# A Fourier mixing layer and a leaky-ReLU feed-forward: the down projection by 20 products per 2x4x3 block

## The chip, the cores and the metric

The kernel runs on one core of a Trainium2 chip, in one launch. The metric is device time in microseconds; the kernel before takes 1897.99 us (median of 3 runs, 1897.3 to 1898.26). Below, PE is TensorE (matrix products), DVE VectorE, ACT ScalarE, POOL GpSimd, and SP the engine whose queue issues most transfers.

## The reference

```python
def _attn_ref(x):                      # x: (8, 3008, 256) float32
    X = np.fft.fft(x, axis=1)
    X = np.fft.fft(X, axis=2)
    return X.real.astype(np.float32)

def _moe_ref(x, w_in, w_out):          # x: (24064, 256), w_in: (256, 2048), w_out: (2048, 256)
    h = x @ w_in
    g = np.maximum(0.01 * h, h)
    return (g @ w_out).astype(np.float32)
```

The result of the first, reshaped to (24064, 256), is the input of the second.

## The kernel before

**Mixing.** The real part of a two-dimensional Fourier transform has symmetries, so for each batch b only a quarter of the frequencies is made by matrix products. `fold_x` adds and subtracts mirrored rows and columns of x on DVE, `fold_rows` splits rows once more (with turns by `angle` on ACT and DVE), `even_rows` and `odd_rows` multiply by cosine and sine tables on PE, and `butterfly` puts the parts together on DVE. The result of a unit (batch b, parity c) are two tiles `mix0` and `mix1`, the cosine and the sine part, of 752 or 753 frequencies each (`UW`). The Fourier transform along the features is folded into w_in once, which gives `wf` (`fold_w_in`), with the weights of one frequency apart in `wn`; that frequency is spread over all partitions in `nb` (`spread`).

**Up.** A unit is cut into 3 blocks of 250 or 251 columns, 48 blocks in all. A step (j, f) takes block j and two of the 16 feature blocks of 128 (f and 8 + f). `raised` (line 820) does 4 matmuls, into PSUM tiles `cos_ps` and `sin_ps`. `activate` adds wn x nb to the cosine part (line 829), then makes cosine + sine and cosine - sine (lines 833 and 834), which belong to two mirrored output columns, all on DVE, and applies the leaky ReLU on ACT (line 835). So a block of 251 columns gives 502 output columns.

**Down.** The first two blocks (`plain = 2`) are multiplied by w_out in the plain way (`down_plain`, line 873), while the weights are still being converted from float64. From the third on, a step is a 2x2x2 block product by 7 products in place of 8: `combine_w_out` makes 4 sums of weights once, the four GpSimd instructions of lines 842 to 845 make 4 sums of the hidden values per step, and `down` does 7 matmuls (line 893) that accumulate over the 8 steps of the block into 7 halves of PSUM banks. At the end of the block, ACT copies one and DVE puts out four results by 7 additions (line 917), and two transfers store them.

**Order.** In the start, up to step 15, the order of all engines is written out by hand (`manual_schedule`). From step 23 on only DVE's is, and for the other engines program order, with a lag of 3 steps between up and down, sets the priorities. `fold_x`, `fold_rows`, `dft` and `spread` for the next unit are hung onto steps by the tables `folds`, `row_folds` and `transforms`.

PSUM has 8 banks: 4 turn round as `up` (also used by the transforms), 4 as `sum`.

Of the kernel before, what the change touches and what calls it, by code (L numbers as in the profile page):

```python
# [16 lines left out]
P = 128  # L67
# [3 lines left out]
NT = 8  # L71
# [24 lines left out]
SLOPE = 0.01  # L96
# [148 lines left out]
def chunks():  # L245


    out, at = [], 0
    for b in range(B):
        for c in PARITIES:  # L250
            for j in range(0, UW[c], CW):
                n = min(CW, UW[c] - j)
                out.append((b, c, j, n, at))
                at += 2 * n
    return out, at


def columns():

    at = np.zeros(B * S, np.int64)  # L260
    for b, c, j, n, first in chunks()[0]:
        col = j + np.arange(n)
        half, k = col >= KW[c], k_order(c)
        k = np.concatenate([k, k[k != Q]])[col]
        plus, minus = np.where(half, H + k, k), np.where(half, H - k, (S - k) % S)
        at[b * S + minus] = first + n + np.arange(n)
        at[b * S + plus] = first + np.arange(n)
    return at
# [3 lines left out]
def tile_fnet_leaky_relu(  # L272
# [16 lines left out]
    PS = bass.MemoryType.PSUM  # L289
    const = ctx.enter_context(tc.tile_pool(name="const", bufs=1))  # L290
    xp = ctx.enter_context(tc.tile_pool(name="xp", bufs=1))
    work = ctx.enter_context(tc.tile_pool(name="work", bufs=1))
    dram = ctx.enter_context(tc.tile_pool(name="dram", bufs=1, space=bass.MemoryType.DRAM))
    ps = ctx.enter_context(tc.tile_pool(name="ps", bufs=1, space=PS))

    def up_ps(name="up_ps"):
        return ps.tile([P, 512], F32, tag="up", bufs=4, name=name)

    def dft_ps():
        return up_ps("dft_ps")  # L300

    def x_tile():
        return xp.tile([LOADED, 2, 2, NT, D], F32, tag="x", bufs=1, name="xt")

    def sum_ps():
        return ps.tile([P, 512], F32, tag="sum", bufs=4, name="sum_ps")

    def load_x(b):
        t = x_tile()
        for h in range(2):  # L310
            for odd in range(2):
                load_rows(t, b, h, odd)
        return t

    def load_rows(t, b, h, odd):
        nc.sync.dma_start(t[:, h, :, odd * NI[0] : NI[0] + odd * NI[1]], x[b, h, odd])
# [4 lines left out]

    zs = {}
# [22 lines left out]
    def fold_x(b, at):  # L345

        t, rows = xs[b], slice(0, NT)
        h, i = divmod(at, 2)
        if h < 2 and i == 0:
            add_mirrors(t, h, rows)  # L350
        elif h < 2:
            for part in range(2):
                fold_columns(t, h, part, rows)
        else:
            fold_halves(t, i, 3 - h, rows)
        if at == 7:
            zs[b] = xs.pop(b)

    def turn(x, y, a, part, tmp, to, v):
# [3 lines left out]
        nc.scalar.activation(tmp[0], y, ACT.Copy, scale=sin)  # L363
        nc.scalar.activation(tmp[1], y, ACT.Copy, scale=cos)
        if v is nc.vector:
            v.scalar_tensor_tensor(to[0], in0=x, scalar=cos, in1=tmp[0], op0=ALU.mult, op1=op[part])
            v.scalar_tensor_tensor(to[1], in0=x, scalar=sin, in1=tmp[1], op0=ALU.mult, op1=op[1 - part])
            return
        nc.scalar.activation(to[0], x, ACT.Copy, scale=cos)
        nc.scalar.activation(to[1], x, ACT.Copy, scale=sin)  # L370
# [3 lines left out]
    class Rows:  # L374
# [3 lines left out]
        def __init__(self, src, scratch, part, c):  # L378
            self.src, self.scratch, self.part, self.c = src[0:ROWS], scratch, part, c

        def z(self, i, n=None):

            block = 16 // len(self.scratch)
# [3 lines left out]
        def fold_even(self, v=nc.vector):  # L387
            x, y, z = self.src[:, 2], self.src[:, 3], self.z
            if self.c == 1:
                turn(x, y, 0, self.part, (z(0), z(1)), (z(6), z(7)), v)  # L390
# [6 lines left out]
        def fold_odd(self, v=nc.vector):  # L397
            x, y, z = self.src[:, 4:6], self.src[:, 6:8], self.z
            if self.c == 1:
                for i in range(2):  # L400
                    turn(x[:, i], y[:, i], 1 + i, self.part, (z(2 + 2 * i), z(3 + 2 * i)), (z(8 + 2 * i), z(9 + 2 * i)), v)
# [3 lines left out]
            else:  # L405
# [5 lines left out]
                turn(z(b), z(b + 1), 0, self.part, (z(8), z(9)), (z(10), z(11)), v)  # L411
                self.odd = z(7 - self.part), z(6 + self.part), z(10), z(11)

    def rows_of_x(b, part, c):

        t = zs[b]
        src = t[:, (c + part) % 2, 0, :, part * P : (part + 1) * P]
        return Rows(src, [t[:, part, 1].rearrange("p c (i d) -> p (c i) d", i=2)], part, c)

    class Direct:  # L420
# [14 lines left out]
        def odd_rows(self, m, lo=0, hi=KW[1]):  # L435

            po, n = dft_ps() if m == P else sum_ps(), KW[1]
# [26 lines left out]
    rows_of = {}  # L464

    def fold_rows(u, part, odd):
        if not odd:
            rows_of[u, part] = rows_of_x(u[0], part, u[1])
            rows_of[u, part].fold_even()
        else:  # L470
            rows_of[u, part].fold_odd()


    feat_sb = const.tile([P, 2, 2 * P], F32, name="feat_sb")
    wf = const.tile([P, 2, F], F32, name="wf")
    wn = const.tile([P, NF], F32, name="wn")
    wo = const.tile([P, 2, NH, D], F32, name="wo")
    wt = const.tile([P, 4, NH, P], F32, name="wt")
    nyx = const.tile([LOADED, 2, 2, NT, B], F32, name="nyx")
    nyz = const.tile([LOADED, 16, B], F32, name="nyz")  # L480
    nyf = const.tile([LOADED, 2, 2, 2 * FI, B], F32, name="nyf")
# [3 lines left out]
    one = const.tile([1, P], F32, name="one")  # L485
    tabs = {}

    def load_tab(n, c):
        t = const.tile([LOADED, TW[c][n % 2]], F32, name=f"tab_{n}_{c}")
        nc.sync.dma_start(t, seq_tab[n, c, :, 0 : TW[c][n % 2]])  # L490
        tabs[n, c] = t
# [4 lines left out]
    class Weights:  # L496
# [7 lines left out]
        def __init__(self, src, dst):  # L504
            tag = RAW[len(parts)]
            bufs = 1 if tag == "raw" else 2
            words = src.shape[1] * src.shape[2]
            self.raw = work.tile([P, 2 * WN], F32, tag=tag, bufs=bufs, name="raw")[:, 0:words]
            self.dst, self.n = dst, dst.shape[1]
            self.f64 = src.dtype != F32  # L510
            raw = self.raw if not self.f64 else self.raw.bitcast(src.dtype)
            nc.sync.dma_start(raw.rearrange("p (c n) -> p c n", c=src.shape[1]), src)
            parts.append(self)
# [4 lines left out]
        def begin(self):  # L518
# [3 lines left out]
            self.power = work.tile([P, WN], F32, tag="power", bufs=2, name="power")[:, 0 : self.n]  # L522
# [40 lines left out]
    def load_w_in(f0, n, blocks=(0, 1)):  # L563
        words, made = w_in.shape[1] // F, []
        for a in blocks:
            w = work.tile([P, WN], F32, tag="win", bufs=4, name="win")[:, 0:n]
# [4 lines left out]
    def fold_w_in(f0, n, made, tag="up", pieces=1, queue=nc.sync):  # L571


        for w in (1, 0):
            m = n // (1 if w else pieces)
            for at in range(0, n, m):
                pt = ps.tile([P, 512], F32, tag=tag, bufs=4, name="wf_ps")[:, 0:m]
# [12 lines left out]
    def load_w_out(q):  # L590

        src = w_out[q * WB * P : (q + 1) * WB * P, :].rearrange("(c p) d -> p c d", p=P)
        h, f = divmod(q * WB, NH)
        return Weights(src, wo[:, h, f : f + WB, :].rearrange("p c d -> p (c d)"))

    def combine_w_out(f):

        b = [[wo[:, h, f : f + WB, i * P : (i + 1) * P] for i in range(2)] for h in range(2)]
        t = [wt[:, i, f : f + WB, :] for i in range(4)]
        for to, x, y in ((t[0], b[0][1], b[0][0]), (t[1], b[1][1], t[0]), (t[2], b[1][1], b[0][1]), (t[3], b[1][0], t[1])):  # L600
            nc.gpsimd.tensor_tensor(to, x, y, op=ALU.subtract)
# [37 lines left out]
    def butterfly(to, m, part, c, v=nc.vector, direct=False):  # L639
# [4 lines left out]
        def tile_of(tag, w, bufs=1):  # L644
            return work.tile([P, w], F32, tag=tag, bufs=bufs, name=tag)

        if not direct or v is not nc.vector:
            od = tile_of("od", 568)
        if v is nc.vector:
            ab, ev = tile_of("ab", KC), tile_of("ev", KC, 2)  # L650
# [14 lines left out]
        def copied(bank, at, w):  # L665

            a = work.tile([P, 384], F32, tag="e0", bufs=2, name="e0")
            if v is nc.vector:
# [28 lines left out]
        def added(po, lo=0, hi=kw):  # L697
            if c == 0:
                for lo, hi in ((0, 189), (189, kw)):
                    at = lo + (lo > 0)  # L700
                    nc.vector.tensor_tensor(to[0:m, lo:hi], ev[0:m, lo:hi], po[0:m, at : at + hi - lo], op=ALU.add)
                return
            nc.vector.tensor_tensor(to[0:m, lo:hi], ev[0:m, lo:hi], po[0:m, 0 : hi - lo], op=ALU.add)

        def subtracted(po, lo=0, hi=kw):
            if c == 0:

                last = 283
                for lo, hi in ((0, 189), (189, last), (last + 1, kw)):
                    at, first = lo + (lo > 0), kw + lo - (lo > last)  # L710
                    nc.vector.tensor_tensor(to[0:m, first : first + hi - lo], ev[0:m, lo:hi], po[0:m, at : at + hi - lo], op=ALU.subtract)
                return
            nc.vector.tensor_tensor(to[0:m, kw + lo : kw + hi], ev[0:m, lo:hi], po[0:m, 0 : hi - lo], op=ALU.subtract)

        def odd(po):
            if c == 1:
# [4 lines left out]
                v.tensor_tensor(to[0:m, 0:kw], ev[0:m, 0:kw], od[0:m, 0:kw], op=ALU.add)  # L721
                v.tensor_tensor(to[0:m, kw : UW[c]], ev[0:m, 0:kw], od[0:m, 0:kw], op=ALU.subtract)
# [8 lines left out]
            v.tensor_tensor(to[0:m, 0:kw], ev[0:m, 0:kw], od[0:m, 0:kw], op=ALU.add)  # L731

            last = 283
            v.tensor_tensor(to[0:m, kw : kw + last], ev[0:m, 0:last], od[0:m, 0:last], op=ALU.subtract)
            v.tensor_tensor(to[0:m, kw + last : UW[c]], ev[0:m, last + 1 : kw], od[0:m, last + 1 : kw], op=ALU.subtract)
# [3 lines left out]
    def mix(u, blk, direct=False):  # L739

        t = work.tile([P, UW[0]], F32, tag=f"mix{blk}", bufs=2, name=f"mix{blk}")
# [425 lines left out]
```

## Time and profile before

| | |
|---|---|
| median of the runs | 1897.99 us (1897.3 to 1898.26) |
| profiled execution: span | 1895.3 us |
| TensorE busy | 1889.2 us, 100% |
| VectorE busy | 1266.8 us, 67% |
| GpSimd busy | 1055.5 us, 56% |
| ScalarE busy | 501.0 us, 26% |
| TensorE's granted clock | 1.000 of full |
| read from and written to HBM | 52.40 MB and 24.71 MB |

The span runs from the first to the last instruction of one profiled execution. A line of the groups gives source line, engine, operation, output and input tiles, shape and count, then the busy time of the group in us and the mean time of one instruction in ns, then the idle time of the engine ahead of it and what ended it. A line of a timeline begins with start and length in us. Each float32 matmul of this kernel has two records.

### The profile page before, as it was taken

The page shows a single profiled execution, that of the slowest core. Times are in us where ns is not written, and L with a number is a line of the kernel's source. Part 1 is how long each engine was busy: PE and PEld are TensorE (multiplying, and loading weights), DVE is VectorE, ACT ScalarE, POOL GpSimd, SP SyncE. Part 2 cuts the span into 40 slices and gives each one's busy share as a digit, 9 for nine tenths or more (in the row PEclk, how much of TensorE's full clock was granted, in tenths as well). Part 3 has the DMA queues.
Part 4 walks back from the last instruction along what each step waited for, and adds up shares of the span by engine and source line. Part 5 has one row for each costly group of instructions (what it writes and reads, how often), then busy time and mean ns, then how long its engine had stood idle before and what let it go on. Part 6 is the DMA issues. An engine that isn't in the chain of part 4 may idle for free.

```text
span 1895.3 us, 25288 instructions
## 1 busy us (share of the span) xinstructions
PE 1889.2 (100%) x9088; PEld 1682.3 (89%) x9088; DVE 1266.8 (67%) x2543; ACT 501.0 (26%) x674; POOL 1055.5 (56%) x1510
## 2 busy tenths in 40 slices
PE   9999999999999999999999999999999999999999
PEld 7888888988889888898888988889888898888987
DVE  8857765776656776568756687567865677656554
ACT  3522322223222222222222232222322223222222
POOL 0236555565555655556555565555655556555554
PEclk9999999999999999999999999999999999999999
DMA  7312000110002000020000200003000020000000
GB/s 252 114 58 82 12 20 22 51 69 12 31 11 104 16 22 20 12 108 18 16 20 12 108 23 11 20 12 119 12 12 19 17 114 12 20 11 23 12 12 23
DMA packets 34349, 78.74 MB, mean 42 GB/s; under 512 B 5536, under 2 KB 20000, under 8 KB 34224
## 3 DMA queue, kind: packets, MB, share of 16 engines
q1 hardware_dynamic: 33792, 76.86, 10.9%
q8 instruction: 73, 1.20, 0.3%
q14 instruction: 52, 0.43, 0.1%
q10 hardware_dynamic: 432, 0.26, 0.0%
HBM read 52.40 MB, written 24.71 MB: 41 GB/s over the span
## 4 chain that ended last, share of the span: by engine, by line
PE 99%; DVE 0%; issue 0%; ACT 0%; DVEq 0%; POOL 0%; POOLq 0%
PE sum_ps L893 58%; PE sin_ps L820 17%; PE cos_ps L820 17%; PE sum_ps L873 3%; PE dft_ps L635 3%; PE wf_ps L579 1%; PE sum_ps L956 1%; PE dft_ps L431 0%; PE dft_ps L440 0%; PE sum_ps L440 0%; PE dft_ps L458 0%; PE dft_ps L453 0%; DVE cos L829 0%; PE sum_ps L788 0%; DVE wo L545 0%
## 5 line engine op out<-in xcount | busy, mean ns | idle before, releaser
L835 ACT ACTIVATE g<-g 128x1004 f32<-128x1004 f32 (+1 forms) x384 | 399.3, 1040 | 1134.6 <-DVE g L834 1114.4
L829 DVE SCALAR_TENSOR_TENSOR cos<-nb,wn,cos_ps 128x251 f32<-128x251 f32 (+1 forms) x768 | 330.5, 472 | 534.1 <-PE cos_ps L820 531.1
L842 POOL TENSOR_TENSOR s<-g 128x251 f32<-128x251 f32 (+1 forms) x368 | 280.5, 762 | 711.4 <-ACT g L835 705.5
L893 PE MATMUL sum_ps<-s,wt 128*128 128x251 f32 (+1 forms) x2208 | 527.6, 374 | 0.0
L893 PEld LDWEIGHTS sum_ps<-s,wt 128*128 128x128 f32 x2208 | 415.9, 188 | 52.3
L820 PE MATMUL cos_ps<-mix,wf 128*128 128x251 f32 (+1 forms) x1536 | 387.8, 374 | 0.0
L820 PE MATMUL sin_ps<-mix,wf 128*128 128x251 f32 (+1 forms) x1536 | 387.8, 374 | 0.0
L893 PE MATMUL sum_ps<-g,wo 128*128 128x251 f32 (+1 forms) x1472 | 372.8, 375 | 0.0
L820 PEld LDWEIGHTS cos_ps<-mix,wf 128*128 128x128 f32 x1536 | 291.2, 190 | 34.2 <-issue 0.5
L820 PEld LDWEIGHTS sin_ps<-mix,wf 128*128 128x128 f32 x1536 | 290.4, 189 | 34.7
L893 PEld LDWEIGHTS sum_ps<-g,wo 128*128 128x128 f32 x1472 | 277.4, 190 | 31.6
L833 DVE TENSOR_TENSOR g<-cos,sin_ps 128x502 f32<-128x502 f32 (+1 forms) x384 | 260.4, 678 | 52.0 <-DVE cos L829 6.5
L845 POOL TENSOR_TENSOR s<-g,s 128x251 f32<-128x251 f32 (+1 forms) x368 | 259.3, 705 | 28.8
L843 POOL TENSOR_TENSOR s<-s,g 128x251 f32<-128x251 f32 (+1 forms) x368 | 271.9, 739 | 0.0
L834 DVE TENSOR_TENSOR g<-cos,sin_ps 128x502 f32<-128x502 f32 (+1 forms) x384 | 257.5, 671 | 0.0
L844 POOL TENSOR_TENSOR s<-g 128x251 f32<-128x251 f32 (+1 forms) x368 | 256.2, 696 | 0.0
L893 PE MATMUL sum_ps<-s,wo 128*128 128x251 f32 (+1 forms) x736 | 215.8, 375 | 0.0
L893 PE MATMUL sum_ps<-g,wt 128*128 128x251 f32 (+1 forms) x736 | 215.7, 375 | 0.0
L893 PEld LDWEIGHTS sum_ps<-s,wo 128*128 128x128 f32 x736 | 139.5, 190 | 16.3
L893 PEld LDWEIGHTS sum_ps<-g,wt 128*128 128x128 f32 x736 | 139.8, 190 | 15.8
L917 DVE TENSOR_TENSOR o<-e,sum_ps 128x251 f32<-128x251 f32 (+1 forms) x180 | 66.0, 408 | 0.0
L873 PE MATMUL sum_ps<-g,wo 128*128 128x251 f32 x256 | 57.1, 374 | 0.5 <-DVE wo L545 0.5
(130 smaller groups left out, 802.8 us busy)
## 6 DMA issues: line engine op xcount, KB each, us to landing
xt<-in_x_dram SPq DMA_DIRECT2D x28, 1024.0 KB, 7.6
out_dram<-o SPq DMA_DIRECT2D x78, 251.0 KB, 2.3
raw<-in_w_in_dram SPq DMA_DIRECT2D x8, 512.0 KB, 5.8
raw<-in_w_out_dram SPq DMA_DIRECT2D x8, 512.0 KB, 4.5
out_dram<-o SPq DMA_DIRECT2D x16, 250.0 KB, 2.1
xt<-in_first_x_dram SPq DMA_DIRECT2D x4, 768.0 KB, 8.4
nb<-nyq_dram SPq DMA_DIRECT2D x8, 376.5 KB, 3.4
nb<-nyq_dram SPq DMA_DIRECT2D x7, 376.0 KB, 4.5
```

The costliest lines, as they stand in the source:

```text
L820: nc.tensor.matmul(pt[blk][:, h * n : (h + 1) * n], lhsT=wf[:, blk, fs[h] * P : (fs[h] + 1) * P], rhs=mixed[b, c][blk][:, at : at + n], st ...
L829: nc.vector.scalar_tensor_tensor(cos[:, hs], in0=spreads[b, c][:, at : at + n], scalar=wn[:, fs[h] : fs[h] + 1], in1=pt[0][:, hs], op0=ALU ...
L833: nc.vector.tensor_tensor(g[:, 0], cos[:, 0 : 2 * n], pt[1][:, 0 : 2 * n], op=ALU.add)
L834: nc.vector.tensor_tensor(g[:, 1], cos[:, 0 : 2 * n], pt[1][:, 0 : 2 * n], op=ALU.subtract)
L835: nc.scalar.activation(g, g, ACT.Lrelu)
L842: nc.gpsimd.tensor_tensor(s1, a[1][0], a[1][1], op=ALU.add)
L843: nc.gpsimd.tensor_tensor(s2, s1, a[0][0], op=ALU.subtract)
L844: nc.gpsimd.tensor_tensor(s3, a[0][0], a[1][0], op=ALU.subtract)
L845: nc.gpsimd.tensor_tensor(s4, a[0][1], s2, op=ALU.subtract)
L873: nc.tensor.matmul(sums[j][d][:, r * n : (r + 1) * n], lhsT=wo[:, fs[h] // NH, fs[h] % NH, d * P : (d + 1) * P], rhs=a[r][h], start=(f == ...
L893: nc.tensor.matmul(sums[j][p], lhsT=still[p], rhs=moving[p], start=(f == 0 and i % 2 == 0), stop=(f == NH - 1), skip_group_check=True)
L917: nc.vector.tensor_tensor(to, x, y, op=ALU.add)
```

## The change

1. **Down projection.** A chunk is now half a unit: 376 or 377 frequencies, hence 753 output columns, treated as 3 parts of up to 251. The 16 feature blocks are 4 groups of 4. Weights (2 x 4 blocks) times hidden values (4 x 3 blocks) is done by 20 products in place of 24; each is 4 matmuls, over the 4 members of a group. `W_SUMS` (16 weight sums, once, on GpSimd), `SUMS` (16 sums of hidden values per chunk, 4 x 251 elements each, on GpSimd), `PRODUCTS` (20, adding into 16 halves of banks) and `COMBINED` (22 additions per chunk on DVE) are lists of the scheme. There are 31 chunks after the two plain blocks; the first holds the 250 columns of unit 0 that are left.
2. **Up projection.** Matmuls are 377 columns wide. wn x nb is written into PSUM ahead by ACT (`seed`), and the matmul adds to it. ACT copies the cosine part out of PSUM, DVE makes sum and difference into the rows of a chunk, and ACT applies the leaky ReLU one step later. cos and sin have two banks each, products 3, the transforms 1.
3. **Order.** From step 16 on, a list of events in order of time sets the order of every engine: feature block f of chunk t at 16 t + 1.2 + f, its sums at `SUMS_AT`, its products from 16 t + 18, 5 matmuls a step. Folds, transforms and combinations wait in a queue (`Later`), and `some` puts out as many in each half-step as a budget lets it (0.8 us of DVE work with both inputs in SBUF, 1.2 us of other DVE work). In the last chunk DVE makes each third sum.
4. **Waits of GpSimd.** Each sum waits for the last DVE instruction with two SBUF inputs issued ahead of it (`gate`, `wait_for_gate`).
5. **Folds of x.** x is loaded by halves into three slots; two of three additions read a copy that ACT has put into PSUM (`by_turns`).
6. **Memory.** Tiles are laid out by hand in a few large tensors, the tables are loaded per transform (`load_tabs`), the DMA scratch is set to 512 bytes.

```diff
+SUMS = [
+    (4, 7, 1, 14.43), (8, 12, 1, 15.4), (8, 7, 1, 16.37), (0, 3, -1, 17.34), (15, 13, -1, 18.31),
...
+SUMS_AT = [x[3] for x in SUMS]
+UP_FROM, DOWN_FROM, PER_STEP = 1.2, 18, 5
+ON_POOL, ON_VECTOR, AHEAD, X_AHEAD, TRANSFORM_FROM, TURNS = 0.8, 1.2, 1, 2, 10, 3
...
-        nc.gpsimd.tensor_tensor(s1, a[1][0], a[1][1], op=ALU.add)
-        nc.gpsimd.tensor_tensor(s2, s1, a[0][0], op=ALU.subtract)
-        nc.gpsimd.tensor_tensor(s3, a[0][0], a[1][0], op=ALU.subtract)
-        nc.gpsimd.tensor_tensor(s4, a[0][1], s2, op=ALU.subtract)
...
-        for i, p in enumerate(turns):
-
-            nc.tensor.matmul(sums[j][p], lhsT=still[p], rhs=moving[p], start=(f == 0 and i % 2 == 0),
-                             stop=(f == NH - 1), skip_group_check=True)
...
+        def by_turns(self, to, x, y, op):
+            self.turn = (self.turn + 1) % TURNS
+            if self.turn == 0:
+                return self.tensor_tensor(to, x, y, op)
+            n = int(np.prod(to.shape[1:]))
+            copy = misc_ps[0 : to.shape[0], 0:n].rearrange("p (a b) -> p a b", a=to.shape[1])
+            self.queue.append((0.0, None, lambda: nc.scalar.copy(copy, y)))
+            self.queue.append(None)
+            self.tensor_tensor(to, x, copy, op)
...
+    def wait_for_gate(ins):
...
+        if gate:
+            tc.add_manual_dep(ins.ins, gate[-1].ins.name,
+                              mybir.DependencyInfo(mybir.DependencyClass.Sync, mybir.DependencyReason.DATA), reason="port")
+            gate.clear()
...
+        def seed(self, f):
+            nc.scalar.activation(cos_ps[f % 2][:, 0 : self.w], columns_of(nb_sb, self.u, self.j, self.w), ACT.Copy, scale=wn[:, f : f + 1])
+
+        def up(self, f):
+            cos, sin = cos_ps[f % 2], sin_ps[f % 2]
+            for i, bank in enumerate((cos, sin)):
+                nc.tensor.matmul(bank[:, 0 : self.w], lhsT=wf[:, i, f * P : (f + 1) * P], rhs=columns_of(mix_sb[i], self.u, self.j, self.w),
+                                 start=(i == 1), stop=True, skip_group_check=True)
...
+            nc.scalar.copy(copy, cos[:, 0 : self.w])
...
+        def sum(self, i, engine=None):
+            x, y, sign, _ = SUMS[i]
+            xa, ya = self.value(x), self.value(y)
...
+            ins = (engine or nc.gpsimd).tensor_tensor(self.value(12 + i), xa, ya, op=ALU.add if sign > 0 else ALU.subtract)
+            if engine is None:
+                wait_for_gate(ins)
...
+        def product(self, q, g):
+            w, v, a = PRODUCTS[q]
...
+            nc.tensor.matmul(to, lhsT=weight(w)[:, g], rhs=self.value(v)[:, g],
+                             start=(first and at == 0), stop=(last and g == 3), skip_group_check=True)
...
+            ins = nc.vector.tensor_tensor(part_of[self.copy[v]][:, 0:n], xa, ya, op=ALU.add if sign > 0 else ALU.subtract)
+            if in_sbuf:
+                gate.append(ins)
...
+            us[pool], us[1 - pool] = min(us[pool], 0.3) + (ON_VECTOR, ON_POOL)[pool], us[1 - pool] - 100.0
+            for part in every:
+                part.make_some(us)
+            folds.emit(us)
...
+            elif kind == 1:
+                every[t].sum(i, nc.vector if t == count - 1 and i % 3 == 2 else None)
+            elif kind == 2:
+                every[t].product(*divmod(i, 4))
...
-    nc = bacc.Bacc("TRN2", target_bir_lowering=False, num_devices=1)
+    nc = bacc.Bacc("TRN2", target_bir_lowering=False, num_devices=1, dynamic_dma_scratch_size=512)
```

## Prediction, made before the result was known

> **What bounds the kernel now.** I read the page's busy shares first, then its chain, then the groups by line, then a timeline of two steps. The page:
>
> ```profile
> span 1895.3 us, 25288 instructions
> PE 1889.2 (100%) x9088; PEld 1682.3 (89%) x9088; DVE 1266.8 (67%) x2543; ACT 501.0 (26%) x674; POOL 1055.5 (56%) x1510
> ...
> PE 99%; DVE 0%; issue 0%; ACT 0%; DVEq 0%; POOL 0%; POOLq 0%
> ```
>
> TensorE carries 99% of the chain, and its list of waits holds 1.6 us in all. No wait can be removed; only TensorE's own work can. A busy matmul row is not a price, since rows overlap (374 ns each, yet the group is busy for less), so I take the price from start to start. Two steps of the timeline:
>
> ```profile
> 1003.83 1.01 PE L820 MATMUL cos_ps<-mix,wf 128*128 128x251 f32 x4
> ...
> 1008.50 1.01 PE L820 MATMUL cos_ps<-mix,wf 128*128 128x251 f32 x4
> ```
>
> One step is 4.67 us and holds 11 matmuls (4 up, 7 down; the trace shows two records for each), so **a matmul of 251 columns costs 424.5 ns**. 46 blocks x 8 steps x 4.67 = 1718.6 us of the 1895.3. For other widths:
>
> ```profile
> 135.59 0.80 PE L453 MATMUL dft_ps<-direct,xt 128*128 128x380 f32 x2
> 136.23 0.81 PE L458 MATMUL dft_ps<-direct,xt 126*128 126x188 f32 x4
> 136.88 1.01 PE L893 MATMUL sum_ps<-g,wo 128*128 128x250 f32 x4
> ```
>
> One matmul of 380 columns takes 0.64 us (135.59 to 136.23), two of about 190 take 0.65. Through 251 and 380 goes a line of 1.67 ns a column plus 5 ns; it gives 0.322 us at 190, as seen. So 377 columns cost 0.635 us, 167 cost 0.284.
>
> **The change on TensorE.** Before, two output chunks of 251 take 8 x 7 down products. After, a chunk holds 753 output columns as 3 parts of 251 and takes 20 products x 4 matmuls. Up: 16 feature blocks x 2 matmuls, now of 377 columns instead of 2 x 251.
> A chunk: 32 x 0.635 + 80 x 0.4245 = 20.3 + 34.0 = 54.3 us. There are 30 of these and a short first one (columns 502 to 752 of unit 0: 32 x 0.4245 + 80 x 0.284 = 36.3). Sum 1664.7 us against 1718.6: **53.9 us less**. The transforms keep their matmuls (448 records of line 635, the same tables), and so do the 16 plain steps. TensorE's floor is 1895.3 - 53.9 = 1841.4.
>
> **Can the others feed it?** A chunk has 16 steps, so a step is 54.3 / 16 = 3.39 us. Per step:
>
> VectorE. Removed: the two scalar_tensor_tensors and the two 502-wide adds. Added: an add and a subtract of 377 with one input in PSUM. Rows: 251 takes 408 ns (line 917), 502 takes 675, hence 542 for 377, twice = 1.08; half of the chunks cut the subtract in two (241 + 441), mean 1.15. Then 22 combining ops of 251 a chunk, 22 x 0.41 / 16 = 0.56, and folds and transforms: all rows of the kind sum to about 290 us before, spread over some 450 steps, 0.6. Together 2.3 us of 3.39.
>
> ScalarE. Removed: one 1004-wide activation per old step. Added: a copy of 377 out of PSUM (368 at 251, 573 at 502, so 0.47); a seed of 377 into PSUM, for which there is no row: at least the PSUM read's 0.47, at most an SBUF activation scaled between 388 ns at 128 and 1040 at 1004, 0.57, which I take since the source is SBUF; a Lrelu of 753, 0.85. With the copies of x through PSUM (16 of 512 a batch, 0.58 each, 0.15 a step), of 3 products a chunk (0.07) and the turns (0.25): 2.3 us of 3.39. It is in order: copy f, seed f+2, Lrelu f-1. cos and sin have two banks each, so up f waits for VectorE's f-2: two steps (6.8 us) less some 2.5 us of work, about 4 us of cover for every VectorE or ScalarE delay. Without that cover each delay falls on TensorE in full.
>
> GpSimd. Removed: 368 x 4 adds of 251. Added: 16 sums a chunk of 4 x 251 = 1004 elements, one a step. No row has this size. The nearest:
>
> ```profile
> L842 POOL TENSOR_TENSOR s<-g 128x251 f32<-128x251 f32 x304 | 240.3, 791 | 560.5 <-ACT g L835 560.5
> L844 POOL TENSOR_TENSOR s<-g 128x251 f32<-128x251 f32 x304 | 207.7, 683 | 0.0
> ...
> L394 POOL TENSOR_TENSOR nyz<-nyx 95x8 f32<-95x8 f32 x1 | 0.2, 202 | 0.0
> ```
>
> By four times an undisturbed row (0.70) a sum takes 2.8 us; that is the upper end, without a fixed part. But 8 elements already take 0.20, so the slope is (0.70 - 0.20) / 243 = 2.06 ns and a sum takes 2.25 us. **The Trainium skill** ("GPSIMD Engine Reference", section 3, Performance versus the Vector engine) measures 4497 ns for 2048 elements and speaks against putting two-input adds there; with the same 0.20 its slope is 2.1 and the sum 2.3. I take 2.25, because the trace itself shows a fixed part. At 2.8 the step still has 0.59 us left; at 2.25, 1.14.
>
> **The wait of the sum for VectorE's batch.** What it answers is in two groups:
>
> ```profile
> L734 DVE TENSOR_TENSOR mix<-ev,od 128x283 f32<-128x283 f32 x14 | 12.9, 922 | 0.0
> ```
> ```profile
> 115.07 0.43 DVE L734 TENSOR_TENSOR nyq<-ev,od 8x283 f32<-8x283 f32 x1
> ```
>
> The same line, 283 elements with both inputs in SBUF, takes 0.43 us with GpSimd idle and 0.92 with it busy; the 512-wide adds with a PSUM input (lines 833 and 834) stay at 0.67 beside the same GpSimd work. The skill ("SBUF — State Buffer", Who interferes with whom) says that the later of the two blocks until the first is done. Applied here it speaks against longer sums: an SBUF-only op that arrives late stands for up to 2.25 us where it stood for 0.5. By it an unordered schedule loses up to 2.25 us in a step; by the row, 0.5. The order by waits makes it neither: batch first, then the sum. Behind a waiting sum on GpSimd there are only later sums, whose products come 2 steps (6.8 us) later. SBUF-only ops are few: per 64 steps 24 combining ops (9.8 us), about 10.6 of transforms and 8 of x (one fold in three, the others read a copy in PSUM), 8 x 0.69 = 5.5; 0.40 us a step. GpSimd's cycle: 0.40 + 2.25 + about 0.15 of two handshakes (0.07 from ScalarE's end to GpSimd's start at 1003.72) = 2.8 of 3.39. Covered, so priced at nothing; if the cover goes, the product two steps on is late.
>
> **Edits with one answer.** The 512 bytes of scratch: nothing, since every transfer goes out by SP or ScalarE queues and none by GpSimd. Between 0 and nothing else. Weight sums: 16 of 512 elements, 1.24 us each, on an idle GpSimd in the plain steps. Tables now loaded per transform (4 x 190 KB a unit, 6.0 us to landing) and x by halves: SP is nearly idle, but its queue is in order: a table load waits for the last matmul reading that table, and behind it stand `spread` and the output stores. The first fold of x is issued 2 steps (6.8 us) after a load that lands in 5.2 to 11.4 us (median 7.6): VectorE stands up to 4.6 us, against 4 us of cover, 14 times; 0 to 8 us, taken as 2. Six stores of 125 KB a chunk take the place of two of 251 per block, and nobody waits for them until the 14 part slots run out.
>
> **What the deeper pipeline costs.** Products trail the ups by 18 steps, where they trailed by 3. *Fill:* in chunk 0's 16 steps TensorE has 13.6 us of ups, two plain downs (3.41 each), the Nyquist rows (1.4) and two direct transforms (2.67 each): 27.1 us. VectorE has four pieces a step (0.32 + 0.23 + 0.23 + 0.32, 17.6), the direct butterflies (14 x 0.33), the Nyquist part (3) and folds (2.7): 28 us; then two steps of chunk 1's ups alone, 1.27 us of matmul beside ScalarE's 1.9. Between 0 and 12 us, taken as 4. *Tail:* 80 products without ups, 2.12 us a step; sums, of which VectorE takes a third, alternate on the port: 2 x 2.25 + 1.2 = 5.7 us in 6.2 of products. 0 to 8, taken as 2; after the last product come three short VectorE ops and a store, as now. *Unit boundaries:* the last butterfly is only just ahead of the first up of 14 units: 0 to 1 us each, taken as 2 in all.
>
> **Sum.** 1895.3 - 53.9 + 4 + 2 + 2 + 2 = **1851.4 us** of profiled span. The median of the runs (1897.99) is 2.7 above the span before, so **1854**.
>
> **Rivals.**
> (a) *Bubbles.* Waits at fill, at x loads and at boundaries reach their upper ends: 12 + 8 + 8 + 14 = 42 less the 10 counted gives 1886 at most, 1878 as a middle. For it: everything is in order on five engines. Against: the 4 us cover.
> (b) *GpSimd becomes the bound*, ending slower. If the four-row access brings the sum to 2.8 us and handshakes and blocked VectorE ops bring the cycle over 3.39, each of 480 steps grows. The gain left is 53.9 - 10 = 43.9 us, so it decides from 3.39 + 43.9 / 480 = 3.48 us a step. 2.8 + 0.4 + 0.15 = 3.35 is just below; 10% more on the sum makes 3.63, and 1854 + 480 x 0.24 = 1969. For it: the row times four. Against: the fixed 0.20.
> (c) *Nothing is lost*: the floor, 1841.4 + 2.7 = 1844.
>
> **How the numbers follow.** Likeliest case with its own range 1845 to 1868: 0.62, (c) being its edge. (a) 1868 to 1893: 0.20. (b): 0.16. No change: 0.02. The range leaves out most of (b) and the top of (a): 1843 to 1887. Within 0.2% (about 3.8 us, what this measurement can tell) is 0.02, faster 0.82, slower 0.16.
>
> **What would show it.** Right: TensorE near 100%, a pitch of 54.3 us a chunk, GpSimd rows of 1004 near 2.25 us, VectorE's SBUF-only rows back to their undisturbed times. Wrong: TensorE waits for sums (b), or for the copied cos and the sin bank (a); matmuls of 377 dearer than 0.635.

## The result, and the profile after

The changed kernel takes 1857.0 us (median of 4 runs, 1855.45 to 1857.02) beside 1897.64 us (1897.19 to 1898.26) for the kernel before in the same comparison: a ratio of 0.9782, 95% interval 0.9768 to 0.9796. The prediction's 1854 is 3 us short. The profiled execution took 1855.2 us from first to last instruction, 40.1 less than before, where the sum of the prediction had 1851.4.

The page of the changed kernel, its busy shares and the engines of its chain:

```profile
span 1855.2 us, 22815 instructions
PE 1840.8 (99%) x7936; PEld 1454.7 (78%) x7936; DVE 1122.9 (61%) x2688; ACT 1081.7 (58%) x1951; POOL 1069.1 (58%) x533
...
PE 93%; DVE 3%; ACT 1%; DMA 1%; issue 1%; POOL 0%; DVEq 0%; SPq 0%; ACTq 0%; POOLq 0%
```

TensorE fell from 1889.2 to 1840.8 us of busy time, 48.4, and from 100% to 99% of the span. The chain that ended last now leaves TensorE for 7% of the span where it was 1%, but most of that isn't lost time: TensorE's own listed waits are some 10 us in all, beside 1.6 before. A step of the timeline, which holds one up of 377 columns on each of cos and sin (two records a matmul) and five products, runs from one line of cos to the next:

```profile
1000.97 0.80 PE L1053 MATMUL cos_psa<-mixc,wf 128*128 128x377 f32 x2
1001.60 0.80 PE L1053 MATMUL sin_psa<-mixs,wf 128*128 128x377 f32 x2
1002.24 2.28 PE L1112 MATMUL sum_psc<-block,wt 128*128 128x251 f32 x10
1004.36 0.80 PE L1053 MATMUL cos_psb<-mixc,wf 128*128 128x377 f32 x2
```

It takes 3.39 us, and a matmul of 377 columns about 0.635 (1000.97 to 1001.60 to 1002.24): both the prediction's. In the windows of the steady part TensorE is busy 50.00 of every 50 us from 250 to 1850 us. The stalls are elsewhere. Its list of waits (us in total, times, longest):

```profile
PE cos_psb L625 <- DVE block L591: 2.1, 1, 2.1
PE cos_psa L1053 <- ACT cos_psa L1048: 2.0, 4, 1.4
PE cos_psa L625 <- DVE block L591: 1.9, 1, 1.9
PE cos_psb L1053 <- ACT cos_psb L1048: 1.4, 4, 0.7
PE sum_psa L1354 <- POOL block L1359: 1.1, 1, 1.1
PE sum_psa L1112 <- POOL block L1095: 0.7, 1, 0.7
```

Lines L625 are products in the start that need a converted piece of w_in; L1053 with L1048 are ups that wait for their seed from ScalarE, all in the fill, the stretch before products stand in every step. The 1.1 us of L1354 stand at the very start, in both kernels. One wait for a sum is 0.7 us, at 185 us, in the products of chunk 0. In the tail, after the last up, TensorE waits for nothing.

The feeding engines, groups with shapes kept apart (busy us, mean ns, then idle ahead and what ended it):

```profile
L1095 POOL TENSOR_TENSOR block<-block 128x1004 f32<-128x1004 f32 x475 | 1017.0, 2152 | 637.6 <-DVE part L1156 207.3 <-DVE xt L932 177.0 <-PE cos_psb L1053 73.3
L1048 ACT ACTIVATE cos_psa<-nb,wn 128x377 f32<-128x377 f32 x240 | 139.0, 579 | 7.8
L1075 DVE TENSOR_TENSOR block<-cos,sin_psa 128x377 f32<-128x377 f32 x240 | 130.2, 543 | 61.2 <-PE sin_psa L1053 38.9 <-ACT cos L1061 21.2 <-POOL block L1095 1.1
L1156 DVE TENSOR_TENSOR part<-part 128x251 f32<-128x251 f32 x180 | 91.2, 520 | 15.1 <-ACT part L1128 15.1
L932 DVE TENSOR_TENSOR xt<-xt 95x256 f32<-95x256 f32 x56 | 31.9, 599 | 0.5
```

A sum takes 2.15 us in the mean and 1.98 in the median (2.25 predicted), a seed 0.58 (0.57), a difference of 377 columns 0.543 (0.542). GpSimd stood 637.6 us idle ahead of its sums, mostly until a VectorE instruction with two SBUF inputs ended: that is the wait that the change put in. VectorE's rows of that kind did not come all the way down to their undisturbed times, as the prediction asked: adds of 251 (L1156) take 0.52 in the mean, where the last one of the kernel, with GpSimd idle, takes 0.41.

**Where the 3.8 us between the sum and the span come from.** Three spots of the trace settle it. First, the start. The same up (step 15) begins at 106.85 us in the kernel before and at 112.87 in the changed one: 6.0 us late, before the new scheme has begun. VectorE and GpSimd in the timeline there:

```profile
55.02 5.58 POOL L651 TENSOR_TENSOR wt<-wo 128x512 f32<-128x512 f32 x4 [17.73 <-DVE wo L591]
...
57.00 1.07 DVE L580 SCALAR_TENSOR_TENSOR block<-block 128x512 f32<-128x512 uint32 x1
...
57.99 1.49 DVE L572 TENSOR_SCALAR block<-block 128x512 int32<-128x512 int32 x1
...
59.40 1.49 DVE L573 TENSOR_SCALAR block<-block 128x512 int32<-128x512 int32 x1
...
64.88 0.42 DVE L572 TENSOR_SCALAR wo<-block 128x512 int32<-128x512 int32 x1
```

While four weight sums run on GpSimd, a TENSOR_SCALAR of VectorE's weight conversion takes 1.49 us, where it takes 0.42 with GpSimd idle (the last line). The next converted piece is late, and TensorE waits for it, once near 65 and once near 88 us. The second wait costs more than its length:

```profile
67.98 1.88 PE L625 MATMUL sin_psa<-block 128*128 128x512 f32 x4
...
86.67 1.02 PE L625 MATMUL cos_psb<-block 128*128 128x512 f32 x2
89.81 1.21 PE L625 MATMUL cos_psb<-block 128*128 128x512 f32 x2 [2.11 <-DVE block L591]
90.81 3.53 PE L625 MATMUL sin_psb<-block 128*128 128x512 f32 x4
```

```profile
84.00:88.00 4.00, 3.70 (x16) 2.56 (x14) 3.86 (x8) 1.97 (x3) 0.00 (x0) 1.00 0.44 131
88.00:92.00 4.00, 2.19 (x4) 1.16 (x5) 3.86 (x9) 1.67 (x3) 0.00 (x0) 0.84 0.00 0
92.00:96.00 4.00, 4.00 (x12) 2.31 (x12) 2.46 (x5) 3.10 (x5) 0.00 (x0) 0.73 0.04 2
96.00:100.00 4.00, 4.00 (x21) 3.57 (x20) 1.26 (x3) 0.34 (x1) 0.00 (x0) 1.00 0.03 0
```

In the windows (length, then busy time of PE, PEld, DVE, ACT, POOL, granted clock, DMA share, GB/s) the granted clock drops to 0.84 and 0.73 after that wait. The four records of sin take 3.37 us from start to start (90.81 to 94.18), where the same four after the first wait, at full clock, take 1.72 (67.98 to 69.70): 1.65 us. With waits of 1.93 and 2.11 that is 5.7 of the 6.0. The length of the wait alone does not decide the dip: after the first one, of 1.93 us, the granted clock stayed at 1.00 here, and in the run with direct folds below, a wait of 1.93 us at the same place was followed by 0.86 and 0.71.

Second, the fill. From 124.77, where the ups of chunk 0 begin, to 154.31, where products fill every step, are 29.54 us. The matmuls in it are worth 23.2 at the prices of the steady part (16 ups 13.6, Nyquist rows 1.4, two direct transforms of 2.56 each, two ups of 377 columns 2.54, products 0.57): 6.3 lost. The end of it in TensorE's timeline, and two instructions of ScalarE there:

```profile
144.87 0.69 PE L1053 MATMUL cos_psb<-mixc,wf 128*128 128x251 f32 x2 [0.19 <-ACT cos_psb L1048]
...
146.17 0.69 PE L1053 MATMUL cos_psa<-mixc,wf 128*128 128x251 f32 x2 [0.19 <-ACT cos_psa L1048]
...
148.00 0.69 PE L1053 MATMUL cos_psb<-mixc,wf 128*128 128x251 f32 x2 [0.72 <-ACT cos_psb L1048]
...
150.53 0.90 PE L1053 MATMUL cos_psa<-mixc,wf 128*128 128x377 f32 x2 [1.41 <-ACT cos_psa L1048]
```
```profile
146.57 0.58 ACT L940 COPY dft_ps<-xt 128x512 f32<-128x512 f32 x1
...
148.97 0.59 ACT L940 COPY dft_ps<-xt 128x512 f32<-128x512 f32 x1 [0.48 <-DVE xt L930]
```

With no products yet to fill the step, ups of 0.85 us follow each other every 1.30 us from 139.66 to 146.17: ScalarE's copy, seed and Lrelu set the pace, and five steps lose 2.3 us. The three steps behind them take 1.83, 2.53 and 2.41 us and lose 3.2: there ScalarE also copies x for the next fold into PSUM (L940), ahead of what the next up waits for.

Third, the products of chunk 0, which are shorter (167 columns, a step of 2.69 us). From 154.31 to 198.99 they and the ups beside them take 44.7 us, at steady prices 43.3: 1.4 lost, about 1.0 of it where TensorE waits for a sum that has itself waited for a fold on VectorE:

```profile
185.56 0.83 PE L1112 MATMUL sum_psa<-block,wo 128*128 128x167 f32 x4 [0.69 <-POOL block L1095]
```
```profile
183.88 1.62 POOL L1095 TENSOR_TENSOR block<-block 128x668 f32<-128x668 f32 x1 [1.16 <-DVE xt L932]
```

So the span is 1841.4 (the floor) + 6.0 (start) + 6.3 (fill) + 1.4 (chunk 0's products) = 1855.1, and 1855.2 was measured.

### The profile page after: what moved, and what is told of

The parts are those of the page before. It is cut to its first block, busy times and chain, and to the rows that moved or that the text cites. A ratio compares the mean times of both kernels' runs of the same rounds, so it can differ in the third digit from the quotient of the medians.

```text
span 1855.2 us, 22815 instructions
## 1 busy us (share of the span) xinstructions
PE 1840.8 (99%) x7936; PEld 1454.7 (78%) x7936; DVE 1122.9 (61%) x2688; ACT 1081.7 (58%) x1951; POOL 1069.1 (58%) x533
## 4 chain that ended last, share of the span: by engine, by line
PE 93%; DVE 3%; ACT 1%; DMA 1%; issue 1%; POOL 0%; DVEq 0%; SPq 0%; ACTq 0%; POOLq 0%
PE sum_psb L1112 18%; PE sum_psa L1112 18%; PE sum_psc L1112 18%; PE cos_psa L1053 8%; PE cos_psb L1053 8%; PE sin_psb L1053 8%; PE sin_psa L1053 8%; PE dft_ps L689 3%; PE sum_psc L911 1%; PE sum_psa L911 0%; PE dft_ps L911 0%; PE sum_psb L911 0%; DVE block L1075 0%; DMA block<-in_w_out_dram 0%; ACT cos L1061 0%
## 5 line engine op out<-in xcount | busy, mean ns | idle before, releaser
L1095 POOL TENSOR_TENSOR block<-block 128x1004 f32<-128x1004 f32 (+1 forms) x491 | 1040.6, 2131 | 689.5 <-DVE part L1156 209.3
L1075 DVE TENSOR_TENSOR block<-cos,sin_psb 128x376 f32<-128x376 f32 (+5 forms) x576 | 251.7, 484 | 383.5 <-PE sin_psb L1053 375.8
L1075 DVE TENSOR_TENSOR block<-cos,sin_psa 128x376 f32<-128x376 f32 (+5 forms) x576 | 251.9, 485 | 271.1 <-PE sin_psa L1053 221.7
L1324 ACT ACTIVATE block<-block 128x753 f32<-128x753 f32 (+1 forms) x494 | 399.7, 809 | 0.1
L1112 PE MATMUL sum_psb<-block,wt 128*128 128x251 f32 (+1 forms) x1336 | 314.4, 372 | 0.0
L1112 PE MATMUL sum_psa<-block,wt 128*128 128x251 f32 (+1 forms) x1328 | 313.5, 372 | 0.0
L1112 PE MATMUL sum_psc<-block,wt 128*128 128x251 f32 (+1 forms) x1304 | 309.7, 373 | 0.0
L1112 PEld LDWEIGHTS sum_psb<-block,wt 128*128 128x128 f32 x1336 | 249.5, 189 | 53.9
L1112 PEld LDWEIGHTS sum_psa<-block,wt 128*128 128x128 f32 x1328 | 248.2, 189 | 54.0
L1112 PEld LDWEIGHTS sum_psc<-block,wt 128*128 128x128 f32 x1304 | 244.5, 189 | 53.4
L1053 PE MATMUL cos_psa<-mixc,wf 128*128 128x377 f32 (+1 forms) x496 | 196.4, 478 | 2.0 <-ACT cos_psa L1048 2.0
L1053 PE MATMUL cos_psb<-mixc,wf 128*128 128x377 f32 (+1 forms) x496 | 196.4, 477 | 1.4 <-ACT cos_psb L1048 1.4
L1053 PE MATMUL sin_psa<-mixs,wf 128*128 128x377 f32 (+1 forms) x496 | 196.1, 477 | 0.0
L1053 PE MATMUL sin_psb<-mixs,wf 128*128 128x377 f32 (+1 forms) x496 | 196.0, 477 | 0.0
L1048 ACT ACTIVATE cos_psa<-nb,wn 128x377 f32<-128x377 f32 (+1 forms) x248 | 142.8, 576 | 8.1
L1048 ACT ACTIVATE cos_psb<-nb,wn 128x377 f32<-128x377 f32 (+1 forms) x248 | 142.7, 576 | 8.1
L1053 PEld LDWEIGHTS sin_psa<-mixs,wf 128*128 128x128 f32 x496 | 93.8, 190 | 61.9 <-DVE block L1075 1.0
L1053 PEld LDWEIGHTS sin_psb<-mixs,wf 128*128 128x128 f32 x496 | 93.7, 190 | 61.9 <-DVE block L1075 0.7
L940 ACT COPY dft_ps<-xt 128x512 f32<-128x512 f32 (+1 forms) x112 | 65.8, 588 | 71.5 <-DVE xt L930 71.5
L1053 PEld LDWEIGHTS cos_psa<-mixc,wf 128*128 128x128 f32 x496 | 93.0, 189 | 14.8 <-ACT cos_psa L1048 4.2
```

The costliest lines, as they stand in the source:

```text
L940: self.queue.append((0.0, None, lambda: nc.scalar.copy(copy, y)))
L1048: nc.scalar.activation(cos_ps[f % 2][:, 0 : self.w], columns_of(nb_sb, self.u, self.j, self.w), ACT.Copy, scale=wn[:, f : f + 1])
L1053: nc.tensor.matmul(bank[:, 0 : self.w], lhsT=wf[:, i, f * P : (f + 1) * P], rhs=columns_of(mix_sb[i], self.u, self.j, self.w), start=(i == ...
L1075: nc.vector.tensor_tensor(row[:, at : at + end - lo], copy[:, lo:end], sin[:, lo:end], op=op)
L1095: ins = (engine or nc.gpsimd).tensor_tensor(self.value(12 + i), xa, ya, op=ALU.add if sign > 0 else ALU.subtract)
L1112: nc.tensor.matmul(to, lhsT=weight(w)[:, g], rhs=self.value(v)[:, g], start=(first and at == 0), stop=(last and g == 3), skip_group_check= ...
```

## The experiments

The theory after the first reading: the gain is TensorE's smaller work, 6 us went in the start to the weight sums beside the conversions, 6 in the fill, and the lag between ups and products covers all other delays. Its rivals: that something else delays the start; and that the cover alone is not enough, so that the kernel stands or falls with the waits of the sums, with the copies of x through PSUM or with GpSimd's speed.

### The weight sums moved behind the plain steps, in one row

```diff
-    SUM_WEIGHTS = {10: (0, 1, 2), 13: (3,)}
+    SUM_WEIGHTS = {}
...
                     nyq_of.append(nyq)
+                    for last in range(4):
+                        sum_weights(last)
```

> The 16 weight sums of GpSimd are moved from plain steps 10 and 13 to behind the Nyquist folds of step 14; nothing else changes. Theory (the start lost time because two batches of these sums, at 55 and 78 us, hold the port that VectorE's conversions need, so two folds of w_in come late and TensorE stands 1.9 and 2.1 us, after which its granted clock dips to 0.73): the waits of line 625 go, the clock stays at 1.00 and the time falls by 4.0 + 1.6 = 5.6 us, 1857.0 to about 1851.4. Rival (the conversions are late for another reason: the new layout of the buffers or their loads): the waits stay and the time is within 1.5 us of 1857.0.

1868.33 us (1868.18 to 1869.46), ratio 0.9843 (0.9828 to 0.9857): about 11 us slower than the changed kernel. The waits of L625 are gone and the up of step 15 begins at 106.46, 6.4 us earlier, so the stalls of the start do go away with the sums. But the gain was lost at once, in another place. GpSimd, VectorE and TensorE in the timeline:

```profile
106.82 19.59 POOL L651 TENSOR_TENSOR wt<-wo 128x512 f32<-128x512 f32 x16
```
```profile
106.29 20.46 DVE L500 TENSOR_TENSOR xt<-xt 128x128 f32<-128x128 f32 x4
126.68 0.85 DVE L885 SCALAR_TENSOR_TENSOR part<-nb,wn,cos_psb 128x251 f32<-128x251 f32 x2
```
```profile
130.09 3.71 PE L911 MATMUL sum_psc<-block,wo 128*128 128x251 f32 x8 [14.97 <-ACT block L891]
```

Four small adds with both inputs in SBUF, 0.90 us in all in the next run, where the weight sums come after them, take 20.46 us. One of the four accounts for it: begun at 106.71, it took 19.84 us, where the median of the four is 0.29. It ended only when the whole row of 16 sums was done, not between two of them. Behind them in VectorE's order stands the activation's input, so TensorE waits 14.97 us; between 120 and 130 us its granted clock is 0.50, and eight records take 3.5 us from start to start in place of 1.7.

### The weight sums in two parts, each behind VectorE's last batch

```diff
-    def sum_weights(last):
+    def sum_weights(lo, hi, after):
...
+            if i == order[lo]:
+                tc.add_manual_dep(ins.ins, after.ins.name,
...
             made[1](odd_rows(nyq_of[0], B))
+            sum_weights(11, 16, last_on_vector[0])
...
                         evens[part].fold_odd(t[:, part, 1, 0:2, 0:P])
+                    sum_weights(0, 11, last_on_vector[0])
```

> The 16 weight sums in two parts, each behind the VectorE work with two SBUF inputs that it would hold up: 11 after the last fold of step 14 (108 us in the run with late sums), 5 after the last butterfly of the Nyquist rows. Theory (a row of sums with no gap between them shuts VectorE's SBUF-only instructions out for the whole row, not for one sum; at 55 and 78 us that costs 4 us of waits of TensorE and a clock dip, in the run with late sums it cost 15): the waits of line 625 are gone, no wait above 3 us appears before the first products, time 1857.0 - 6 = about 1851. Rival (wherever the 20 us of sums stand in the start they cost as much): 1856 or more.

1851.0 us (1850.67 to 1851.41), ratio 0.9755 (0.974 to 0.9769), span 1849.2. GpSimd's rows, the first timeline, start right after VectorE's batches and stop before the next one; in the second, the up of step 15:

```profile
107.64 13.53 POOL L652 TENSOR_TENSOR wt<-wo 128x512 f32<-128x512 f32 x11 [0.43 <-DVE xt L500]
123.31 6.20 POOL L652 TENSOR_TENSOR wt<-wo 128x512 f32<-128x512 f32 x5 [2.15 <-DVE block L791]
```
```profile
106.81 1.01 PE L880 MATMUL cos_psb<-mixc,wf 128*128 128x251 f32 x4
```

The up begins at 106.81 (106.85 in the kernel before), and the span falls by 6.0 us, what the start had cost. The fill is as long as it was (118.70 to 148.26). That the loss in the start comes from the sums beside the conversions is shown by this pair of runs: the same sums, moved and ordered by a wait, cost nothing.

### The fill's TensorE work spread over more of chunk 0

```diff
-        if r < 2:
-            down_plain(*steps[14 + r])
-        if r == 2:
+        if r in (2, 4):
+            down_plain(*steps[14 + (r - 2) // 2])
+        if r == 6:
...
-        if r in (4, 7):
-            dft_direct((r - 4) // 3)
+        if r in (8, 11):
+            dft_direct((r - 8) // 3)
```

The two late plain products read hidden values that chunk 0's first steps have already written over, since they share memory; amount and kind of work are the same.

> In the first 16 steps of the event list the two last plain downs go from steps 0 and 1 to 2 and 4, the Nyquist rows from 2 to 6, the two direct transforms from 4 and 7 to 8 and 11. The work is the same. Theory (the fill is paced by ScalarE at 1.3 us a step, and TensorE's other work of 13.5 us stands ahead of the ups instead of between them): TensorE's gaps between 139 and 153 us shrink from about 6 to about 2 us, time about 1853. Rival (the fill is held by latencies from engine to engine, or by VectorE, so that the order does not matter): 1856 to 1858; if the later Nyquist rows make the first seeds of chunk 1 late, over 1858.

1861.59 us (1861.25 to 1862.12), ratio 0.9806 (0.9791 to 0.9821): slower, not faster. A new stall appears in the direct transform, in TensorE's timeline, with the windows of that place:

```profile
137.75 1.44 PE L483 MATMUL dft_ps<-block,xt 128*128 128x378 f32 x6
143.11 1.61 PE L505 MATMUL sum_psa<-block,xt 128*128 128x380 f32 x2 [3.92 <-issue]
```
```profile
140.00:142.00 2.00, 0.00 (x0) 0.00 (x0) 0.20 (x1) 0.00 (x0) 0.00 (x0) 1.00 1.03 423
142.00:144.00 2.00, 0.89 (x2) 0.62 (x3) 0.00 (x0) 0.00 (x0) 0.00 (x0) 0.71 0.98 401
144.00:146.00 2.00, 2.00 (x7) 1.70 (x6) 0.00 (x0) 0.00 (x0) 0.00 (x0) 0.50 0.22 84
```

For 3.9 us TensorE stands, for the last 2.9 of them (140.2 to 143.1) no engine works, and the 16 DMA engines are full with a load of x at over 400 GB/s; then the granted clock is 0.71 and 0.50. "issue" says that the profile shows nothing that TensorE waited for. Instructions fetched behind the load would look like this, but no run separates it. The 3.9 us, and about 1.5 more for the direct transform at the low clock, are more than the 4.6 us by which the kernel is slower, so the spreading itself brought a microsecond at most, and this run decides little on the fill beyond one point: the late ups are still 1.3 us and more apart behind ScalarE.

### Without the waits of the sums

```diff
-            if engine is None:
-                wait_for_gate(ins)
+            gate.clear()
```

> The sums of GpSimd no longer wait for VectorE's batch. Theory of the prediction (two steps of cover swallow what the port costs): VectorE's SBUF-only rows get longer by up to 2 us each, and the time stays within 4 us of 1857.0. Rival (without the order the port makes VectorE or GpSimd late for TensorE): 10 us or more slower, 1867 to 1890, with TensorE waiting for the seeds or for the sums.

1873.23 us (1872.6 to 1873.38), ratio 0.9866 (0.985 to 0.9883), span 1871.5: 16 us slower than with the waits. TensorE's waits and VectorE's groups:

```profile
PE sin_psb L1053 <- DVE block L1075: 7.1, 9, 2.7
...
PE sin_psa L1053 <- DVE block L1075: 2.1, 7, 0.7
```
```profile
L1155 DVE TENSOR_TENSOR part<-part 128x251 f32<-128x251 f32 x180 | 203.8, 1145 | 9.0 <-ACT part L1127 9.0
...
L932 DVE TENSOR_TENSOR xt<-xt 95x256 f32<-95x256 f32 x56 | 99.4, 1803 | 0.5
```

The SBUF-only adds go from 520 to 1145 ns and from 599 to 1803; VectorE's busy time rises from 1122.9 to 1419.2 us. The lag hides most of these 296 us, but not all: TensorE waits 9.2 us for VectorE's sums and differences out of the sin banks, and part of the rest is its granted clock after a wait (0.83 between 210 and 220 us). About half of the 16 us falls early: the same up of chunk 2 begins at 209.07 with the waits and at 217.42 without, 8.4 us later. So the cover alone is not enough, and the waits of the sums are worth 16 us.

### Folds of x without the copies through PSUM

```diff
-ON_POOL, ON_VECTOR, AHEAD, X_AHEAD, TRANSFORM_FROM, TURNS = 0.8, 1.2, 1, 2, 10, 3
+ON_POOL, ON_VECTOR, AHEAD, X_AHEAD, TRANSFORM_FROM, TURNS = 1.2, 1.2, 1, 2, 10, 1
```

> All folds of x are done by VectorE with both inputs in SBUF, none over a copy in PSUM; the budget of SBUF-only work is raised from 0.8 to 1.2 us a step so that they fit. The sums wait for the batch as before. Theory (GpSimd's cycle is 0.4 + 2.0 + 0.15 us a step on the mean; the 16 folds more of 0.6 us a batch raise 0.40 to 0.55, but up to 1.5 us in the steps with folds, where the cycle is then 3.65 of 3.39 us, made good by the steps after): within 6 us of 1857.0, ScalarE's busy time down by 66 us. Rival (the copies through PSUM are what keeps GpSimd in time): 10 us or more slower, TensorE waits for sums.

1855.67 us (1855.0 to 1856.33), ratio 0.9775 (0.976 to 0.9789): no difference from the changed kernel that its interval can tell. ScalarE's busy time falls from 1081.7 to 1023.2 us, VectorE's rises from 1122.9 to 1146.7. With the waits in place the copies buy nothing. The run also tells something of the fill, since ScalarE has no copies of x there. Its two longest waits for a seed (0.72 and 1.41) are gone, but TensorE now waits for VectorE, whose direct folds stand in the same steps:

```profile
150.88 0.90 PE L1053 MATMUL sin_psa<-mixs,wf 128*128 128x377 f32 x2 [1.66 <-DVE block L1075]
```

The fill takes 30.2 us (124.08 to 154.30) beside 29.5. So lightening ScalarE there did not shorten it; moving the folds of x out of those steps was not tried. The split weight sums and direct folds together:

> The split weight sums, and all folds of x by VectorE from SBUF with the budget of 1.2 us. Theory (the two edits act in different stages, 1.3 us by the folds at most): about 1850, within 2 us of the run with the split alone. Rival (the copies through PSUM only seemed to cost nothing, because the start hid it): 1854 or more.

1850.36 us (1850.19 to 1850.77), ratio 0.9751 (0.9735 to 0.9767): 6.6 us below the changed kernel; nearly all of it is the weight sums.

### More work on GpSimd

After every sum of hidden values, one or two adds of 192 elements on a buffer of their own:

```diff
             if engine is None:
                 wait_for_gate(ins)
+            if engine is None:
+                nc.gpsimd.tensor_tensor(spare, spare, spare, op=ALU.add)
```

> One GpSimd addition of 192 elements in a buffer of its own follows each sum. Theory (GpSimd's cycle is 0.4 + 2.0 + 0.15 = 2.6 us of 3.39; the addition costs 0.2 + 192 x 0.0021 = 0.6 us, together 3.2): the time stays within 6 us of 1857. Rival (GpSimd has no such room, since its sums wait for batches that come late in the step): 1870 or more, with TensorE waiting for sums.

With one: 1857.37 us (one run), span 1855.3, GpSimd at 70%, the add 0.53 us. No loss.

> Two such additions follow each sum. Theory (2.6 + 1.2 = 3.8 us against 3.39, so GpSimd sets the pace, and the prediction's break-even of 3.48 us a step is passed): 480 x 0.4 = some 190 us more, 1990 to 2080, slower than the kernel before. Rival (cycles overlap with the batches of VectorE, and there is room yet): under 1900.

With two: 1861.7 us (one run), span 1859.8, GpSimd at 85%. The expectation of a kernel bound by GpSimd (1990 us and more) was wrong by over 100 us. Its timeline:

```profile
1000.15 1.97 POOL L1096 TENSOR_TENSOR block<-block 128x1004 f32<-128x1004 f32 x1
...
1003.12 2.32 POOL L1096 TENSOR_TENSOR block<-block 128x1004 f32<-128x1004 f32 x1
...
1006.45 2.33 POOL L1096 TENSOR_TENSOR block<-block 128x1004 f32<-128x1004 f32 x1
```

The cycle is 3.0 to 3.33 us, below the step's 3.39, and TensorE is busy 1200 of 1200 us between 400 and 1600. That expectation rested on the prediction's cycle, which adds VectorE's batch (0.40) and handshakes (0.15) to the work of GpSimd in every step; in these lines the sum and both adds nearly fill the cycle, and little is left for a batch of its own. That it runs beside the added instructions is the likely reading, and it pays for it (the adds of L1156 with both inputs in SBUF rise from 0.52 to 0.72 us in the mean); which of them it overlaps was not measured. The loss of about 4.6 us is nearly all in four waits near both ends of the run, longer or new: three for sums (1.5 us where the changed kernel has 0.7, and 1.6 and 0.6 in the last chunk) and 1.2 for VectorE in the sin bank.

## Why the prediction was right

**TensorE's floor: right.** The step (3.39), the price of 377 columns (0.635) and so the 53.9 us came as worked out: with the floor of 1841.4 the losses found in the trace add up to the span within 0.1 us. Reading prices from start to start, not from busy time, is what made it so: busy time fell by 48.4 only.

**Can the others feed it: right, with room.** The rows for sum, seed, copy (0.47 predicted, 0.473) and difference stand within 5% in the mean, the Lrelu at 0.816 for 0.85. The slope with a fixed part (2.25) was nearer than four times the row (2.8), whose rival (b) needed a step over 3.48; even 1.0 us more work a step did not get there.

**The wait of the sum: right in direction.** It leaves no loss in the steady part, and without it the kernel loses 16 us. It was not quite free: priced at nothing, it costs about 1.0 us once, in chunk 0's products. Of the two prices for an unordered schedule, VectorE's mean loss was near the one from the row, 0.5 us a step (296 us over some 480 steps are 0.6), while single groups stood for much longer (1.80 us in place of 0.60). As far as the run with two more adds shows, the 0.40 us a step for the batch was too high as an addition to GpSimd's cycle.

**Weight sums: wrong, 6.0 us in place of 0.** The step that failed is "Weight sums: 16 of 512 elements, 1.24 us each, on an idle GpSimd in the plain steps". The sums themselves were priced well (1.35), and GpSimd was idle. But what such a sum does to VectorE, which the prediction weighed for the hidden sums, was put at nothing here: VectorE, converting weights in those steps, had no slack. The rule as the prediction words it, instructions with two SBUF inputs, would have caught only part of it (L580, 1.07 us for 0.69). The largest delays were in TENSOR_SCALAR rows with one tensor input (L572 and L573, 1.49 for 0.42).

**Fill: a size off, 6.3 for 4,** inside the 0 to 12 given. The prediction set TensorE's 27.1 us in chunk 0 beside VectorE's 28 as totals and had no line for ScalarE there. But TensorE's other work came first, and the late ups then ran at ScalarE's 1.30 us. The first two ups of chunk 1, put at 1.9 us of ScalarE each, came 2.53 and 2.41 us after the one before, with the copies of x. (A direct transform is 2.57 in the kernel before, from 134.31 to 136.88, not 2.67; that moves the 27.1 by 0.2.)

**x loads and unit boundaries: 0 for 2 + 2; tail: 0 for 2.** TensorE has no wait in any of them. The allowance for these 6 us is what hid the missed 6.0 of the start: that the total is so near is partly luck, since errors cancel (6.0 + 2.3 + 1.4, less 6). The median stands 1.8 above the profiled span where 2.7 was taken.

**Rivals.** (a) had bubbles at x loads and boundaries: none. Bubbles of its kind came at the fill and once in chunk 0's products. (c), nothing lost, missed by 13 us. The scratch of 512 bytes was not run alone.

## What to carry to other kernels

A price of "nothing, the engine is idle" needs a second look at whom that engine holds up: here the cost of idle GpSimd's work fell on VectorE, and from there on TensorE. Where two engines hold each other up, order them by a wait, batch after batch, and keep a row of instructions on one short, since the other may wait for the whole row. And when a deep pipeline replaces a shallow one, price the fill step by step by its slowest feeder, because the work that hid it in the steady part isn't there yet.

## What the runs showed of the hardware

- A VectorE add with both inputs in SBUF did not get in between consecutive instructions of GpSimd: beside a row of 16 sums (19.59 us) one add took 19.84 us, where the median of its group of four is 0.29.
- VectorE's one-input conversions (TENSOR_SCALAR of 512 int32) were held as well: 0.42 us alone, 1.49 beside weight sums.
- With a TensorE wait of 2.1 us the granted clock was 0.84 and 0.73 in two windows of 4 us, which cost 1.65 us on top of the 2.1; in a wait of 15 us it was 0.50. A wait of 1.93 us left it at 1.00 in one run and brought 0.86 and 0.71 in another.
- In one run TensorE stood for 3.9 us, all engines for 2.9 of them, with no wait in the profile, beside a transfer of 423 GB/s; the cause is open.
